# A spectral filter and a gated feed-forward block on one core: written order with a framework scheduler, against an order planned at build time

## The chip, the cores and the metric

One of the eight cores of one Trainium2 chip. The metric is the device time of one execution in microseconds (us); medians are over the executions of a run. "Span" is the time from the first to the last instruction of the profiled execution; in every execution on record it is 1.7 to 1.9 us shorter than the time of that execution. Engine names are those of the profile: PE is TensorE's matmul, PEld its weight load, DVE is VectorE, ACT is ScalarE, POOL is GpSimd, SP is SyncE, which here only issues DMA (SPq is its queue).

## The reference

Inputs are drawn in bfloat16. What matters:

```python
x  = A_x                                     # 1 x 2048 x 640
xn = layernorm(x)                            # over the 640
X  = rfft2(xn) * (w_r + 1j * w_i)            # over both axes
s  = irfft2(X)                               # back to 2048 x 640
g  = silu((gelu(xn @ w_gate) * (xn @ w_up)) @ w_down)   # 640 -> 1536 -> 640
return x + s * g
```

## The kernel before

The 2048 rows are treated as 16 slabs of 128. Each slab is normalised (`stats`, `apply`), turned so that the 640 columns lie on partitions (`turn`), and folded (sums and differences with the mirrored half), which halves the work of the Fourier transform. The transforms are matmuls with small tables. The folded slabs are stored in DRAM and read back regrouped. Then come eight "spectral" steps, a second trip through DRAM (`reload`), and sixteen inverse steps. All this is interleaved with the feed-forward block, which runs in four groups of four slabs: 12 gate/up tiles, then 4 down projections.

The parts that the change touches:

```python
# one slab at a time
def turn(n1, eng=nc.scalar):
    pt = psum.tile([P, 5, P], BF16, tag="sp", name="pt")
    for c in range(5):
        nc.tensor.transpose(out=pt[:, c, :], in_=xn[:, c * P:c * P + P], identity=ident)   # five PE matmuls
    ...                                                       # one evacuation to xnT, ACT or DVE

def fold(n1):
    ...
    nc.vector.tensor_tensor(out=eo[:, 0, :], in0=xn[:, 0:320], in1=xn[:, 639:319:-1], op=ALU.add)
    nc.vector.tensor_tensor(out=eo[:, 1, :], in0=xn[:, 0:320], in1=xn[:, 639:319:-1], op=ALU.subtract)
    ...                                                       # two more of the same size: xf
    nc.tensor.matmul(pa[:, 0, :], lhsT=F1T, rhs=xf[:, :, 0:128], ...)
    nc.tensor.matmul(pa[:, 1, 0:128], lhsT=F1T, rhs=xf[:, :, 128:160], ...)
    nc.scalar.copy(out=A, in_=flat(pa)[:, 0:D])
    nc.sync.dma_start(out=D2[:, n1, :], in_=A)                # store for the regroup

def inverse(n1):                                              # rows of 644 columns
    ...                                                       # 4 matmuls of 128 columns, then
    nc.tensor.matmul(pvf[0:64, 512:640], lhsT=U[:, 256:320], rhs=I1T, ...)
    nc.tensor.matmul(pvf[64:128, 512:640], lhsT=U[:, LP + 257:LP + 321], rhs=I1T, ...)

def down(n1):
    ph = sp_tile("ph")                                        # both halves in one "sp" PSUM tile
    ...                                                       # 24 matmuls of 320 columns, tanh, multiply
# the order is written by hand: what goes with feed-forward step i
for i in range(12):
    after[i].append((norm, 4 + i))                            # stats, apply, turn
    while nf * 12 < (i + 1) * 16:
        after[i].append((fold, nf)); nf += 1
after[11] += [(gather, 0), (gather, 1), (regroup,)]
for G in range(8):
    after[14 + 2 * G].append((spectral_a, G)); after[17 + 2 * G].append((spectral_b, G))
after[31].append((reload,))
...
```

SP and POOL run what they are given in the written order; PE, DVE and ACT get their order from the framework's scheduler, working from this written sequence. PSUM (the matmul outputs) has two slots each of the tags `sp`, `pg` and `pu`.

## Time and profile before

| | before |
|---|---|
| time, median of 3 runs | 235.64 us (235.01 to 235.66) |
| span of the profiled run | 233.3 us |
| granted TensorE clock, mean | 1.000 |
| PE / DVE / ACT busy | 210.0 / 148.6 / 115.9 us |
| first / last matmul starts | 7.9 / 228.4 us |
| matmuls (columns/2.4 + 2.5 ns each), summed | 200.8 us |

The last line needs a word. PE's busy time overstates the array's work, because matmuls overlap in the records. Back to back, a 512-column matmul starts 0.216 us after the one before and a 320-column one 0.136 us, that is columns/2.4 + 2.5 ns. The Trainium skill, "TensorE: Matmul & The Clock Gate", section "Wait — 56ns, not 53.3ns?", gives the same rule, and the trace agrees. I call the sum of it over all matmuls the **stream**: 1428 matmuls, 200.8 us. (The trace holds 1406 of them; the count is the program's.) Then the time can be taken apart: 7.9 us before the first matmul, 200.8 us of stream, some 20 us of **holes** in which nothing streams, 4.7 us after the last matmul.

From the page of the kernel before, the busy table's line and PE's row of 40 slices (busy tenths):

```profile
PE 210.0 (90%) x1406; PEld 122.1 (52%) x1428; DVE 148.6 (64%) x357; ACT 115.9 (50%) x183; POOL 58.9 (25%) x98
...
PE   0588799899999999999999998999999999999972
```

The same by stage, from the windows view of the kernel before (busy us and instructions of each engine in each stretch, then the granted clock, the DMA engines' mean busy share and GB/s):

```profile
core 0: us, PE busy (x) PEld busy (x) DVE busy (x) ACT busy (x) POOL busy (x), PEclk, DMA share, GB/s
0.00:20.00 20.00, 9.99 (x79) 7.21 (x81) 10.60 (x35) 10.18 (x21) 6.63 (x19) 1.00 0.87 282
20.00:60.00 40.00, 36.38 (x224) 17.71 (x225) 30.21 (x97) 26.41 (x46) 16.69 (x32) 1.00 0.67 223
60.00:100.00 40.00, 39.21 (x279) 23.74 (x283) 29.21 (x55) 24.16 (x32) 22.45 (x27) 1.00 0.41 127
100.00:140.00 40.00, 38.95 (x261) 23.91 (x264) 26.50 (x46) 16.94 (x24) 6.17 (x8) 1.00 0.24 69
140.00:180.00 40.00, 38.46 (x268) 22.53 (x272) 24.05 (x61) 18.89 (x30) 4.29 (x8) 1.00 0.37 128
```

The waits view of the kernel before names what PE stood waiting for (total us, times, longest):

```profile
PE pt L270 <- DVE xn L263: 10.6, 7, 7.9
...
PE pa L289 <- DVE xf L287: 1.6, 4, 0.6
...
PE ph L469 <- DVE G_2846 L458: 1.5, 1, 1.5
...
PE pv L404 <- DMA BU<-D_93: 1.1, 1, 1.1
```

The first line holds the start (7.9 us before the first turn) and six further waits of turns for normalised slabs. `pa <- xf` are folds that came late. The 1.5 us is the last down projection, which waits for an `sp` slot; the 1.1 us is the first inverse step waiting for the reload. Without the start, all PE waits that the view lists add up to 9.9 us. The rest of the 20 us it doesn't name.

### The profile page before, as it was taken

To read this page: it belongs to the slowest core of one execution; us is meant where nothing else is said; L and a number is where in the kernel's file an instruction comes from. 1 tells how busy PE (TensorE), PEld (TensorE's weight loads), DVE (VectorE), ACT (ScalarE), POOL (GpSimd) and SP (SyncE) were. 2 spreads that over 40 slices of the span, in tenths; PEclk is the share of its full clock that TensorE was granted. 3 is DMA by queue.
4 is the path that set the end of the run, shared out by engine and by line. 5 is a ranking of instruction groups with operands and counts; after the bars stand their busy time and mean duration, and the time that the engine had idled before them with its cause. 6 is when DMAs were issued, how large, how long until landed. Compare 5 with 4: busy or idle time off the path is not lost. (4 is left out here: it accounts for less than half of the span.)

```text
span 233.3 us, 3865 instructions
## 1 busy us (share of the span) xinstructions
PE 210.0 (90%) x1406; PEld 122.1 (52%) x1428; DVE 148.6 (64%) x357; ACT 115.9 (50%) x183; POOL 58.9 (25%) x98
## 2 busy tenths in 40 slices
PE   0588799899999999999999998999999999999972
PEld 0363344346755556555666643544666654545751
DVE  2659798872239998688957242976654586544372
ACT  4279877474174655865352424745243464443210
POOL 1531413437733486646000000110100010000000
PEclk9999999999999999999999999999999999999999
DMA  6995994824960332326201039251211123000011
GB/s 190 385 340 134 357 377 149 300 88 95 342 212 16 100 101 64 106 88 159 83 3 45 11 91 408 86 154 59 84 46 41 56 70 101 0 0 0 32 61 52
DMA packets 21091, 29.67 MB, mean 127 GB/s; under 512 B 2368, under 2 KB 18640, under 8 KB 20944
## 3 DMA queue, kind: packets, MB, share of 16 engines
q1 hardware_dynamic: 18592, 23.83, 29.9%
q0 software_dynamic: 2336, 5.26, 8.5%
q10 hardware_dynamic: 144, 0.33, 0.4%
q8 instruction: 11, 0.18, 0.3%
q14 instruction: 8, 0.07, 0.1%
HBM read 21.53 MB, written 7.88 MB: 126 GB/s over the span
## 5 line engine op out<-in xcount | busy, mean ns | idle before, releaser
L440 PE MATMUL pg<-xnT,Wg 128*128 128x512 bf16 (+1 forms) x241 | 63.4, 373 | 1.6 <-DVE xnT L272 1.3
L440 PE MATMUL pu<-xnT,Wu 128*128 128x512 bf16 (+1 forms) x237 | 61.0, 372 | 0.7 <-issue 0.2
L469 PE MATMUL ph<-Wd,u 128*128 128x320 bf16 x384 | 53.8, 299 | 2.5 <-DVE G_2846 L458 1.5
L469 PEld LDWEIGHTS <-u 128*128 128x128 bf16 x384 | 37.4, 98 | 18.0 <-issue 3.3
L448 DVE TENSOR_TENSOR u<-pu,ge 128x512 bf16<-128x512 f32 x48 | 32.9, 685 | 9.4 <-PE pu L440 9.1
L446 ACT ACTIVATE ge<-pg 128x512 bf16<-128x512 f32 x48 | 28.9, 602 | 17.9 <-PE pg L440 17.7
L440 PEld LDWEIGHTS <-Wu 128*128 128x128 bf16 x250 | 24.0, 99 | 22.5
L479 POOL DMA_DIRECT2D xr<-in_A_x_dram x16 | 8.7, 548 | 104.9 <-DVE res L485 104.9
L457 ACT ACTIVATE th<-ph 128x640 f32<-128x640 f32 (+1 forms) x17 | 11.4, 673 | 47.3 <-PE ph L469 47.3
L440 PEld LDWEIGHTS <-Wg 128*128 128x128 bf16 x250 | 22.9, 98 | 20.8 <-issue 0.9
L311 POOL DMA_INDIRECT W<-in_A_w_r_dram,LANE x16 | 16.8, 1047 | 6.0 <-POOL W L308 3.5
L311 POOL DMA_INDIRECT W<-in_A_w_i_dram,LANE x16 | 16.0, 1000 | 4.9 <-issue 4.9
L270 PE MATMUL pt<-ident,xn 128*128 128x128 bf16 x80 | 7.4, 231 | 10.6 <-DVE xn L263 10.6
L411 ACT CAST Vt<-pv 128x640 bf16<-128x640 f32 x16 | 11.1, 692 | 9.0 <-PE pv L408 9.0
L272 ACT COPY xnT<-pt 128x640 bf16<-128x640 bf16 x14 | 9.7, 693 | 10.9 <-PE pt L270 10.9
L353 ACT CAST E<-pe 128x644 bf16<-128x644 f32 x16 | 13.1, 890 | 3.4 <-PE pe L351 3.4
L270 PEld LDWEIGHTS <-xn 128*128 128x128 bf16 x80 | 5.2, 103 | 14.6 <-DVE xn L263 14.2
L242 DVE BATCH_NORM_STATS2 st<-X 128x6 f32<-128x320 bf16 x22 | 10.1, 480 | 3.5 <-DMA X<-in_A_x_dram 3.5
L292 ACT CAST A<-pa 128x640 bf16<-128x640 f32 x16 | 11.1, 693 | 2.5 <-PE pa L290 1.1
L255 POOL TENSOR_SCALAR rstd<-mva 128x1 f32<-128x1 f32 x11 | 3.0, 275 | 31.4 <-DVE mva L243 31.3
L356 DVE TENSOR_TENSOR V<-E 128x644 bf16<-128x644 bf16 x8 | 4.0, 495 | 11.0 <-ACT E L353 11.0
L385 PE MATMUL pi<-R,BD 128*128 128x322 bf16 x64 | 10.5, 300 | 0.4 <-DVE R L377 0.4
(177 smaller groups left out, 269.3 us busy)
## 6 DMA issues: line engine op xcount, KB each, us to landing
D_93<-IU SPq DMA_DIRECT2D x8, 322.0 KB, 2.9
BU<-D_93 SPq DMA_DIRECT2D x4, 644.0 KB, 6.2
D_92<-A SPq DMA_DIRECT2D x16, 160.0 KB, 2.2
BU<-D_92 SPq DMA_DIRECT2D x4, 640.0 KB, 6.9
xr<-in_A_x_dram POOLq DMA_DIRECT2D x16, 160.0 KB, 2.5
out_dram<-res SPq DMA_DIRECT2D x15, 160.0 KB, 1.8
Wg<-in_B_w_gate_dram SPq DMA_DIRECT2D x4, 480.0 KB, 7.6
Wu<-in_B_w_up_dram SPq DMA_DIRECT2D x4, 480.0 KB, 7.7
```

The costliest lines, as they stand in the source:

```text
L242: nc.vector.bn_stats(out=st[:, g, :], in_=x[:, 320 * g:320 * g + 320])
L270: nc.tensor.transpose(out=pt[:, c, :], in_=xn[:, c * P:c * P + P], identity=ident)
L292: nc.scalar.copy(out=A, in_=flat(pa)[:, 0:D])
L311: nc.gpsimd.indirect_dma_start(out=W[:, pm, ri, 0:L], out_offset=None, in_=wsrc, in_offset=bass.IndirectOffsetOnAxis(ap=LANE[:, 2 * G + pm ...
L353: nc.scalar.copy(out=E[:, ri].rearrange("p r (i q) -> p r q i", q=2), in_=pe[:, :, 0:LP].rearrange("p r (q i) -> p r q i", q=2))
L385: nc.tensor.matmul(pi[:, pq, 0:LP], lhsT=BD[:, G, ro, ri, :], rhs=R[:, ri, pq, :], start=(ri == 0), stop=(ri == 1))
L411: nc.scalar.copy(out=flat(Vt), in_=pvf[:, 0:D])
L440: nc.tensor.matmul(ps[:, lo:hi], lhsT=w[:, c, t * P:(t + 1) * P], rhs=xnT[:, c, grp * 512 + lo:grp * 512 + hi], start=(c == 0), stop=(c == ...
L446: nc.scalar.activation(out=ge, in_=pg, func=ACT.Gelu_apprx_tanh)
L448: nc.vector.tensor_tensor(out=u, in0=pu, in1=ge, op=ALU.mult)
L457: nc.scalar.activation(out=th[:, a:b], in_=ph[:, a:b, 0:320], func=ACT.Tanh, scale=0.5)
L469: nc.tensor.matmul(ph[:, a, 0:320], lhsT=uT[grp, t][:, j * P:(j + 1) * P], rhs=Wd[:, t, 320 * a:320 * a + 320], start=(t == 0), stop=(t == ...
```

## The change

Its intent: PE's order should never put a matmul in front of data that isn't there yet. All tasks are entered in a list with their costs in ns, their dependencies and their buffers ("slots"); a scheduler in the build runs through simulated time, gives each free engine the ready task of best rank, and the instructions are then emitted in that order, on every engine, with the framework's scheduling off. With it come smaller changes of the operations:

- slabs 4 to 15 are turned by the DMA crossbar (`dma_start_transpose`) in place of five PE matmuls and an evacuation;
- folds and unfolds work on pairs of slabs, half as many DVE instructions of twice the size;
- the inverse rows have 640 columns, so the tail needs one matmul in place of two;
- a down projection is two halves that use `pg` and `pu` slots, not `sp`; an evacuation goes to ACT or DVE, whichever the plan finds free;
- a few more go along: two more slabs' statistics go to ACT, the first two gate/up tiles are done in four parts, and a pair of folds is stored at once.

The core of the diff, cut:

```diff
+class Plan:
+    MARGIN = dict(PE=250, DVE=60, ACT=60, POOL=60, SP=60)
+    ...
+    def run(self):
+        left, now, order = list(self.tasks), 0.0, []
+        while left:
+            ...                                   # ready task of best rank on a free engine, else step time on
+            occ, lat = t.engs[e]
+            self.free[e] = now + occ
+            t.done = now + lat
+            if t.size:                            # a transfer: one shared wire, 340 bytes per ns
+                self.wire = max(self.wire, now + occ + 900) + t.size * t.slow / 340.0
+                t.done = self.wire + 1000
+            ...
+def c_pe(*ns):
+    occ = sum(n / 2.4 + 2.5 for n in ns)
+    return occ, occ + 240
+...
+    BUFS = dict(sp=2, pg=2, pu=2, s1=4, ma=2, mb=2, mc=2, Y=1, ...)
+...
+    def turn_dma(n1, ap):
+        turned[n1] = add(lambda e: nc.sync.dma_start_transpose(out=xnT[:, :, n1 * P:(n1 + 1) * P],
+                                                               in_=sxn.tile[:, n1 % 2, :]),
+                         "SP", (600, 600), (0, -1, n1), after=[ap], use=[sxn], size=163840, slow=1.6)
+    def fold(j, aps):                             # a pair of slabs; outputs mc, one store per pair
+        nc.vector.tensor_tensor(out=eo.tile[:, :, 0, :], in0=sxn.tile[:, :, 0:320], in1=sxn.tile[:, :, 639:319:-1], op=ALU.add)
+        ...
+        stored[j] = dma(lambda: D2[:, 2 * j:2 * j + 2, :], lambda: A.tile, (0, -1, j), 327680, after=outs, use=[A], slow=1.1)
+...
+        (turn_pe if n1 < 4 else turn_dma)(n1, aps[n1])
-    after[31].append((reload,))
-    ...                                           # the written order
+    with tc.manual_schedule():
+        for t in plan.run():
+            t.emit(t.on)
```

## The prediction

It was written before the changed kernel ran.

> **What bounds the kernel now.** TensorE. The page's busy table gives PE 210.0 of 233.3 us (DVE 148.6, ACT 115.9). Busy overstates the array's work: in the chain that ended last, five 512-column matmuls take 1.08 us and 24 of 320 columns 3.26 us, that is columns/2.4 + 2.5 ns each, which agrees with the Trainium skill, "TensorE: Matmul & The Clock Gate", section "Wait — 56ns, not 53.3ns?". Summed over the program this gives an estimated 201 us of stream. The other 32 us: some 11.5 us of delay by 17 us (7.9 before the first PE instruction in the timeline, then slabs' turns); an estimated 8 us between 17 and 60 us, where the windows by stage show PE at 84 to 96%, DVE at 85 to 94%, DMA at 60 to 90%, and PE waits for xn (turns) and xf (folds); 1.1 us at the reload (140 us); small bubbles; 1.5 us in the last down projection, waiting for a PSUM slot; 4.6 us after the last matmul.
>
> **What the change removes.** 60 of 80 PE turn matmuls (60 x 56 ns = 3.3 us of stream), 12 evacuations of 0.69 us, one 128-column matmul per inverse slab (0.9 us). Stream falls to about 196.6 us. Folds on pairs: 64 DVE operations of 0.32 us become 32 of 0.49 us, about -5 us of DVE. Statistics: 2 slabs (about 2 us each) move from DVE to ACT. Down halves use the pg/pu slots, not sp, so the 1.5 us wait goes.
>
> **What it adds.** 12 crossbar turns of 160 KB. The skill, "DMA: Bandwidth & Descriptors", "Latency and other measured facts", gives 261 GB/s: 0.6 us each plus some 2 us to landing; no run here shows it yet. They queue behind all loads (10.8 MB, at the windows' 290 GB/s done near 37 us). Slabs 4-7 are needed only when group 0 is finished, near 57 us, so I expect no wait. The stores for the regroup stand behind the last turns; the regroup is needed near 72 us. Splitting down adds 16 small tanh and multiply operations, off the path.
>
> **The plan's costs** match the trace: successive 644-element DVE operations start 0.41 us apart, 1288-element ones 0.74, u products 0.60. So DVE should keep up with the static order.
>
> **Sum.** PE reaches its first full-width tile at about 17 us as before, with 6.7 us of stream done; 190 remain; stalls and bubbles after that I put at 6 us (the 16 of before less most of the early 8 and the last 1.5); last matmul near 213; tail 4.3; span 217 to 218, plus the 2.3 us between span and time. Predicted **220 us, 213 to 229**; faster by over 2%: 0.90, within 2%: 0.07, slower: 0.03.
>
> **What would show it right.** 20 turn matmuls, 80 inverse first-stage matmuls; PE busy near 201 us or below; PE at 95% or more in every window from 20 to 60 us; no wait of gate/up for xnT by DMA; no PE gap at the regroup; the last down without a gap.
>
> **What would make it wrong.** Crossbar turns far slower than 160 KB per 1 us, or holding the queue, so that group 1 waits for xnT or the first spectral matmul for the regroup (a 5 to 15 us PE gap near 57 or 72 us); PE waiting in order for R or evacuations in the spectral and inverse stages, if the greedy plan packs them too closely (3 to 5 us); a later start.

## The result, and the profile after

| | before | after |
|---|---|---|
| time, median of 4 runs each, same chip | 235.39 us | 217.77 us (217.3 to 219.55) |
| ratio | | 0.9269 (95%: 0.9229 to 0.9308) |
| span | 233.3 us | 216.1 us |
| first / last matmul starts | 7.9 / 228.4 us | 8.3 / 210.9 us |
| stream | 200.8 us | 196.6 us |
| holes between first and last matmul | 19.8 us | 6.2 us |
| after the last matmul | 4.7 us | 5.0 us |

A ratio is the mean time of one kernel's fast runs over that of the other's of the same rounds, so it is not quite the ratio of the medians quoted. Executions over 1.5% slower than the fastest of the same kernel are left out of the means. The span's gain of 17.2 us is 4.2 us of stream and 13.6 us of holes (2.6 of them the inverse tail's, see e1r_pe_turns), less 0.3 us of later start and 0.3 us of longer tail.

From the page of the changed kernel:

```profile
PE 200.2 (93%) x1392; PEld 123.2 (57%) x1392; DVE 146.3 (68%) x304; ACT 113.0 (52%) x192; POOL 59.0 (27%) x95
...
PE   0499999996999999999999999999999999999991
```

Its windows view, in the same stretches:

```profile
0.00:20.00 20.00, 11.22 (x116) 9.30 (x117) 14.06 (x39) 12.41 (x26) 10.52 (x33) 1.00 0.95 302
20.00:60.00 40.00, 37.77 (x220) 20.80 (x218) 30.70 (x68) 18.39 (x37) 18.14 (x27) 1.00 1.03 259
60.00:100.00 40.00, 40.00 (x282) 23.79 (x280) 25.41 (x46) 21.10 (x30) 8.22 (x7) 1.00 0.29 93
100.00:140.00 40.00, 40.00 (x265) 24.21 (x264) 29.39 (x56) 25.29 (x39) 15.13 (x16) 1.00 0.38 109
140.00:180.00 40.00, 40.00 (x337) 27.68 (x336) 32.29 (x72) 27.01 (x46) 6.43 (x12) 1.00 0.47 157
```

From 60 us to 180 us the view shows no gap of PE. DVE has 146.3 us of work where it had 148.6, and ACT 113.0 where it had 115.9, so the other engines do hardly less; whether the gain is the order's, the experiments must tell. What remains is the digit 6 in PE's row, a hole at 51 us, with a small one at 56 us. The PE timeline of the changed kernel around it (start, duration, then in brackets the idle time and its releaser):

```profile
50.24 0.98 PE L793 MATMUL pu<-Wd,uT 128*128 128x320 bf16 x6
53.12 0.38 PE L470 MATMUL sp<-mb,F1T 128*128 128x512 bf16 x1 [1.90 <-ACT mc L301]
...
56.60 0.38 PE L470 MATMUL sp<-mb,F1T 128*128 128x512 bf16 x1 [0.34 <-ACT mc L301]
```

A fold matmul waits for ACT to free a PSUM slot by evacuating into `mc`. Its waits view says what ACT waited for, and shows one wait near the end:

```profile
ACT mc L301 <- DMA D<-mc: 7.3, 3, 3.7
...
PE sp L470 <- ACT mc L301: 2.2, 2, 1.9
...
DVE ge L817 <- ACT th L802: 1.1, 1, 1.1
```

`mc` has two buffers, and ACT waits until an earlier one has been stored. The timeline of SP's queue in the changed kernel shows where these stores were:

```profile
35.16 8.89 SPq L434 DMA_TRANSPOSE xnT<-s  x6
44.15 0.53 SPq L308 DMA_DIRECT2D D<-mc  x1
44.77 2.58 SPq L434 DMA_TRANSPOSE xnT<-s  x2
47.44 0.53 SPq L308 DMA_DIRECT2D D<-mc  x1
48.06 3.00 SPq L434 DMA_TRANSPOSE xnT<-s  x2
51.16 8.20 SPq L308 DMA_DIRECT2D D<-mc  x4
```

They stood behind crossbar turns. The 16 DMA engines were full at that time, too: in the windows view their busy share between 40 and 50 us is 1.10, and 0.23 in e1r_pe_turns, which has no crossbar turns. So a turn costs its queue and the DMA engines, and the runs below don't separate the two. The changed kernel's view of the turn's line gives its price: duration on the queue as min/median/max, and the time from issue to landing.

```profile
L434 SPq DMA_TRANSPOSE xnT<-s x12: 1227/1250/2228, 31.0 to 49.5; - x12
...
DMA to landing us min/median/max: 3.6/5.2/6.1
```

The plan had reckoned with 600 ns of the queue and 0.77 us of the wire (163,840 bytes times 1.6 over 340).

### The profile page after: what moved, and what is told of

The parts are those of the page before. It is cut to its first block, busy times and chain, and to the rows that moved or that the text cites. A ratio compares the mean times of both kernels' runs of the same rounds, so it can differ in the third digit from the quotient of the medians.

```text
span 216.1 us, 3756 instructions
## 1 busy us (share of the span) xinstructions
PE 200.2 (93%) x1392; PEld 123.2 (57%) x1392; DVE 146.3 (68%) x304; ACT 113.0 (52%) x192; POOL 59.0 (27%) x95
## 4 chain that ended last, share of the span: by engine, by line
PE 89%; DMA 4%; DVE 3%; ACT 2%; issue 1%; SPq 0%; ACTq 0%
PE pg L750 24%; PE pu L750 24%; PE pg L793 11%; PE pu L793 10%; PE sp L650 4%; DMA D<-mc 2%; PE sp L587 2%; PE sp L683 2%; PE sp L696 2%; PE sp L583 2%; PE sp L693 2%; DMA X<-in_A_x_dram 2%; PE sp L566 2%; PE sp L470 1%; DVE STAT L382 1%; PE sp L416 1%
## 5 line engine op out<-in xcount | busy, mean ns | idle before, releaser
L766 DVE TENSOR_TENSOR uT<-pu,ge 128x512 bf16<-128x512 f32 x48 | 32.9, 688 | 40.5 <-PE pu L750 34.9
L793 PEld LDWEIGHTS <-uT 128*128 128x128 bf16 x384 | 36.3, 98 | 13.3
L793 PE MATMUL pg<-Wd,uT 128*128 128x320 bf16 (+1 forms) x192 | 31.6, 301 | 0.0
L793 PE MATMUL pu<-Wd,uT 128*128 128x320 bf16 (+1 forms) x192 | 31.0, 297 | 0.0
L526 POOL DMA_INDIRECT WF<-in_A_w_r_dram,LANE x16 | 17.3, 1083 | 41.7 <-DVE mc L622 37.2
L301 ACT CAST ma<-sp 128x644 bf16<-128x644 f32 (+1 forms) x32 | 24.1, 794 | 4.8 <-PE sp L696 2.6
L526 POOL DMA_INDIRECT WF<-in_A_w_i_dram,LANE x16 | 16.0, 999 | 4.9 <-issue 4.6
L301 ACT CAST IU<-sp 128x640 bf16<-128x640 f32 x16 | 10.9, 693 | 3.3 <-PE sp L650 2.2
L301 ACT CAST Vt<-sp 128x640 bf16<-128x640 f32 x15 | 10.4, 692 | 4.1 <-PE sp L683 4.1
L650 PE MATMUL sp<-R,BD 128*128 128x320 bf16 x64 | 11.1, 300 | 0.0
```

The costliest lines, as they stand in the source:

```text
L301: return nc.scalar.copy(out=out, in_=in_) if e == "ACT" else nc.vector.tensor_copy(out=out, in_=in_)
L526: nc.gpsimd.indirect_dma_start(out=sw.tile[:, pm, ri, 0:L], out_offset=None, in_=wsrc, in_offset=bass.IndirectOffsetOnAxis(ap=LANE[:, 2 * ...
L650: nc.tensor.matmul(pt[:, pq, 0:320], lhsT=BD[:, G, ro, ri, :], rhs=sR.tile[:, ri, pq, pq:pq + 320], start=(ri == 0), stop=(ri == 1))
L766: nc.vector.tensor_tensor(out=u.tile, in0=pu.tile, in1=ge.tile, op=ALU.mult)
L793: nc.tensor.matmul(ps.tile[:, 0:hi - lo], lhsT=uT[grp, t].tile[:, j * P:(j + 1) * P], rhs=Wd[:, t, lo:hi], start=(t == 0), stop=(t == 11))
```

## The experiments

Theory 1: the gain is the planned order with realistic durations; the new operations matter less, and the crossbar turns hardly at all, because the hole at 51 us gives back what they save. Rival 2: the cheaper operations make the gain, and the old order with them would do nearly as well. Rival 3: any static order with enough buffers does it; the timing is beside the point.

The trials used several chips. On chip 14 the kernel before takes what it took at first (235.3 and 235.9 us; one of its executions took 564.91 us and is left out of the ratios). On chips 7 and 8 it takes 242.4 and 244.5 us, and every kernel traced there has stretches in which PE is slow; those runs are told too, but carry little.

### On chip 7: four kernels, three rounds each

**e1_pe_turns** turns all slabs on PE again:

```diff
-        (turn_pe if n1 < 4 else turn_dma)(n1, aps[n1])
+        turn_pe(n1, aps[n1])
```

> The changed kernel with all 16 slabs turned on the TensorE again (evacuated by ACT or DVE as the plan likes), the plan made anew. Theory O (the timed order closes the holes; the crossbar only takes 60 matmuls off the TensorE and costs the 2.5 us hole near 51 us, where stores stand behind turns in the SP queue): 217.8 + 3.3 - 2.5 = about 218.6 us, range 217.5 to 220, with under 1 us of TensorE holes after 20 us. Theory L (the lighter work closes the holes: without PE turns ACT, DVE, PSUM slots and TensorE are free in the first 60 us): 222 us or more, with several us of holes again between 20 and 60 us.

Measured: 235.93 us, ratio to before 0.9750 (0.9708 to 0.9792).

**e2_plan_old_ops** keeps the plan, turns all slabs on PE and also takes back the pairs and the single tail matmul: each pair operation becomes two per slab, with costs to match, and the tail is two matmuls again:

```diff
-            nc.vector.tensor_tensor(out=eo.tile[:, :, 0, :], in0=sxn.tile[:, :, 0:320], in1=sxn.tile[:, :, 639:319:-1], op=ALU.add)
+            for q in range(2):
+                nc.vector.tensor_tensor(out=eo.tile[:, q, 0, :], in0=sxn.tile[:, q, 0:320], in1=sxn.tile[:, q, 639:319:-1], op=ALU.add)
 # ... and so for all eight fold and unfold operations
-                for c in range(5):
+                for c in range(4):
 # ...
+                for q in range(2):
+                    nc.tensor.matmul(pt[64 * q:64 * q + 64, 512:640], lhsT=U[:, 256 + 64 * q:320 + 64 * q], rhs=I1T, ...)
```

> The plan with the old operations: all turns on the TensorE, every fold and unfold operation of a pair split into two of one slab (64 + 64 operations of 320 elements as before), six matmuls in the inverse's first stage. Only the order, the buffers and the split down projection are then new. Theory O: 217.8 + 3.3 + 0.9 - 2.5 = 219.5 to 221 us. Theory L: 226 us or more, most of the way back to 235.

Measured: 243.99 us, ratio 1.0052 (0.9993 to 1.0111).

**e3_before_new_ops** is the kernel before, in its written order, with the new operations: crossbar turns, pairs, 640-column rows, down halves in `pg`/`pu`:

```diff
     def turn(n1, eng=nc.scalar):
         xn = xn_of[n1]
+        if n1 >= 4:
+            return nc.sync.dma_start_transpose(out=xnT[:, :, n1 * P:(n1 + 1) * P], in_=xn)
 # ... fold and unfold on pairs, five inverse matmuls:
-        ph = sp_tile("ph")
+        for a, tag in ((0, "pg"), (1, "pu")):
+            ph = psum.tile([P, 512], FP32, tag=tag, name=tag)
```

> The kernel before, in its own written order, with the new operations: crossbar turns from slab 4, folds and unfolds on pairs, 640-column rows with five matmuls, the down projection in two halves on the gate/up PSUM slots. Theory O: the stream falls by the same 4.1 us, the 1.5 us wait of the last down projection goes, the other holes mostly stay: 226 to 231 us. Theory L: 220 us or less.

Measured: 234.86 us, ratio 0.9699 (0.9666 to 0.9732).

**e4_mc4** is the changed kernel with four `mc` buffers (`mc=2` to `mc=4`), against the hole.

> The changed kernel with four instead of two buffers for the folds' results (the tiles that the stores to DRAM read, which stand behind crossbar turns in the SP queue), the plan made anew. Theory O: the TensorE hole of 2.1 + 0.5 us at 51 to 57 us closes, 215.3 us, range 214.8 to 216.2. Rival: the stores' lateness itself sets the time, the hole only moves to the regroup: 217.8 us as now.

Measured: 231.13 us, ratio 0.9520 (0.9469 to 0.9571); one of its four executions (235.31 us) was slow.

All four came out slower than the same or the nearest kernel did elsewhere, and so did the kernel before, by 7 us. Their traces have stretches (about 45 to 68 us and, in three of the four, 100 to 136 us) where PE's matmuls and weight loads come some 0.7 us or more apart, with nothing to wait for; the timeline of e4_mc4 shows it:

```profile
48.57 0.30 PE L793 MATMUL pu<-Wd,uT 128*128 128x320 bf16 x1 [1.68 <-issue]
48.59 0.10 PEld L793 LDWEIGHTS <-uT 128*128 128x128 bf16 x1 [1.32 <-issue]
...
49.28 0.30 PE L793 MATMUL pu<-Wd,uT 128*128 128x320 bf16 x1 [0.41 <-issue]
```

"issue" means that the profile shows no wait. It is not every engine: in this stretch ACT and DVE do nothing until it is over, but POOL's gathers of the filter weights keep their pace of one in 1.25 us. The granted clock also fell to half in or after such stretches (from 50.7 to 57.6 us in e4_mc4). In all these traces, and in e8_turn_cost_only, each stretch begins during a run of twelve or more such gathers and ends at most 5 us after it (e4_mc4: gathers from 36.2 to 51.3 us, stretch from 47 to 55 us). On chip 14 the same runs of gathers pass without one, so this is a lead and no cause: what causes the stretches stays open. Since they hit the kernels in different places, I don't compare these four.

### On chip 14: the same question again

**c1_after** is the changed kernel unaltered, as a control.

> Control: the changed kernel unaltered, because the last four runs were on a chip on which the kernel before took 242.4 us instead of 235.4[...]. If this chip is like the first: 217.8 us and a ratio to before of 0.927. If it is like the second: ratio near 0.95 and the same stretches.

Measured: 217.74 us, ratio 0.9206 (0.9116 to 0.9295; the interval is wide because it rests on three fast executions of 215.31, 217.61 and 217.87 us; the fourth, 219.09, counts as slow). The hole is there: 1.9 us at 48.1 us and 1.1 us at 52.2 us.

**e2r_plan_old_ops**, the plan with the old operations.

> The plan with the old operations once more, beside the control. Theory O (order closes the holes): 2 to 3 us over the control, 219.5 to 221 us on a chip like the first. Theory L (lighter work closes them): 9 us or more over the control.

Measured: 222.24 us, ratio 0.9452 (0.9410 to 0.9494). That is 4.5 us over the control: more than theory O gave (2 to 3), and half of what theory L asked for (9 or more). Where the extra comes from is told at e1r_pe_turns. From its page, PE's row:

```profile
PE   0589999999999999999999999999999999999990
```

DVE and ACT have more work here than in the kernel before (152.7 and 116.8 us against 148.6 and 115.9), and yet PE has no single hole above 0.4 us after 20 us. So it isn't lighter work that closes the holes.

**e3r_before_new_ops**, the old order with the new operations.

> The old order with the new operations once more, beside the control. Theory O: 226 to 231 us on a chip like the first, 8 to 13 us over the control. Theory L: at most 3 us over it. (On the second chip it was 0.970 of before.)

Measured: 230.54 us, ratio 0.9799 (0.9755 to 0.9843), as theory O had it; whether it is a full 2% faster than before stays unclear. From its page PE's row, and from its waits view:

```profile
PE   0488878888979899999999998999999999999992
```

```profile
PE pa L301 <- DVE xf L296: 6.7, 8, 1.1
...
PE pzt L334 <- DMA BU<-D: 1.3, 1, 1.3
```

All eight pairs of folds now hold PE for about a microsecond each, where before four of the single folds held it for 1.6 us in all. The pair operations are cheaper for DVE, but a pair is ready later, and the order had not been adapted. The two runs and the two kernels themselves make a table of two by two (us):

| | old operations | new operations |
|---|---|---|
| old order | 235.3 | 230.5 |
| planned order | 222.2 | 217.7 |

The order is worth 12.8 to 13.0 us, the operations 4.5 to 4.7 us, and the two add. Rival 2 is refuted. (The columns aren't perfectly clean: the down halves in `pg`/`pu` stayed in the upper right and the lower left kernel, so the removal of the last down's 1.5 us gap counts with whichever came first. And "planned order" stands for all that the plan decides: the order on every engine, the buffers, and which engine takes an evacuation or a slab's statistics. How much each of these is worth isn't separated.)

**e6_all_four** tries four repairs on the changed kernel at once: `mc=4`; the plan's first load landing later (`self.wire` 2200 to 4400 ns); fifteen matmuls on a zero tile before the data arrive, and statistics of slabs 3 to 5 held back so that the first turns come first; the last down's twelve matmuls in one piece per half.

```diff
-        self.wire = 2200.0
+        self.wire = 4400.0
-    BUFS = dict(..., mc=2, ...)
+    BUFS = dict(..., mc=4, ...)
+        pw = psum.tile([P, 512], FP32, tag="pg", name="pg")
+        for _ in range(15):
+            nc.tensor.matmul(pw, lhsT=WARM[:, 0:P], rhs=WARM, start=True, stop=True, ...)
-            for k in range(0, 12, 6):
+            for k in range(0, 12, step_k):            # 12 for the last down
```

> The changed kernel with four edits at four places, to be read one by one in the trace: (1) four buffers for the folds' results: the hole of 2.1 + 0.5 us at 51 to 57 us goes; (2) 15 matmuls on a tile of zeros before the first slab, so that the TensorE is at full clock when the first turns come: the 3.4 us at half speed after 10 us go, 1.0 to 1.8 us; (3) the first slab normalised before the fourth slab's statistics, and the plan told the measured time of the first loads: first turn 0.5 to 0.8 us earlier; (4) the last down projection one column half after the other: tail 0.5 to 0.9 us shorter. Sum: 4 to 6 us under the control, about 213 us on a chip like the first. If starting earlier is worth nothing because DVE sets the pace until 18 us, (2) and (3) together give under 0.5 us.

Measured: 213.86 us, ratio 0.9088 (0.9051 to 0.9126), so 3.9 us below the control. In its trace the hole at 51 us is gone, but a new one of the same size came at 62 us; the PE timeline of e6_all_four:

```profile
61.56 1.24 PE L752 MATMUL pg<-xnT,Wg 128*128 128x512 bf16 x5
64.50 1.07 PE L568 MATMUL sp<-T,BU 128*128 128x128 bf16 x16 [1.70 <-DMA BU<-D]
```

With more `mc` buffers the plan believed that the stores, and so the regroup, would be done much earlier, and put the first spectral matmuls 8.6 us of stream earlier than in the changed kernel (5.4 us if the fifteen matmuls on the zero tile, 3.2 us, are counted in). But the stores still stood behind turns that take longer than the plan thought. The wait had moved to the next step that depended on the same wrong number. (The profiled execution was the slowest of six, 215.52 us; four took 213.5 to 213.9 us, and whether they had this hole isn't known.) The start did improve: five 128-column matmuls start 0.28 us after one another from the first, where the changed kernel needs 0.53 us until 13.4 us, and the first full-width gate tile comes at 16.0 us in place of 18.3.

### On chip 14: the turns, the timing, the turn's cost (five rounds each)

**e1r_pe_turns**, all turns on PE, planned.

> The changed kernel with all turns on the TensorE, once more, hopefully on a chip like the first. Crossbar alone: it takes 3.3 us of matmuls away and brings the hole of 2.0 to 2.6 us near 50 us, so undoing it costs 0.7 to 1.3 us: 218.5 to 219 us, ratio to before about 0.930, with no hole over 0.5 us after 20 us. If the crossbar also frees what keeps the TensorE fed: 221 us or more.

Measured: 217.84 us, ratio 0.9244 (0.9216 to 0.9272): the same as the changed kernel, and a little under the 218.5 to 219 expected. With 3.3 us more of matmuls it has no hole above 0.25 us after 20 us. The crossbar turns are worth nothing here: what they save on PE comes back as a hole of 2.5 to 3 us.

This run also tells what the other operations are worth. It differs from e2r_plan_old_ops only in the pairs and in the tail of the inverse step, and is 4.4 us faster. The PE timelines of e2r_plan_old_ops and then of e1r_pe_turns, one inverse step each:

```profile
150.39 0.39 PE L685 MATMUL sp<-I1T,BU 128*128 128x128 bf16 x4
150.71 0.25 PE L688 MATMUL sp<-I1T,BU 128*64 128x128 bf16 x2
150.88 0.99 PE L804 MATMUL pu<-Wd,uT 128*128 128x320 bf16 x6
...
149.91 0.44 PE L683 MATMUL sp<-I1T,BU 128*128 128x128 bf16 x5
150.19 0.98 PE L793 MATMUL pu<-Wd,uT 128*128 128x320 bf16 x6
```

Four full matmuls and two with 64 columns of weights (`128*64`) hold PE for 0.50 us, five full ones for 0.28 us. The two half ones start 4 ns after one another, but 0.15 us pass before the pair and 0.18 us after it. The kernel before shows the same 0.50 us in its inverse steps. So one matmul in place of two is worth 0.217 us a slab and 3.5 us in all: 0.9 us of stream, as predicted, and 2.6 us of what the sum of the stream leaves in the holes. This is read from the trace; a run with the tail alone changed was not made. It is most of the 4.5 us that the operations are worth under the planned order.

**e5_untimed** keeps the plan's mechanism, ranks and buffers, but lies to it about the durations: every task of an engine costs the same, and transfers take 2 us whatever they move and whatever else is under way.

```diff
-            occ, lat = t.engs[e]
+            occ, lat = {"PE": (900, 1140), "DVE": (500, 620), "ACT": (800, 940), "POOL": (1000, 1150), "SP": (430, 430)}[e]
-                self.wire = max(self.wire, now + occ + 900) + t.size * t.slow / 340.0
-                t.done = self.wire + 1000
+                t.done = now + occ + 2000
```

> The changed kernel planned by the same scheduler with the same priorities, dependences and buffers, but without the timing: every task of an engine counts as equally long (TensorE 0.9, DVE 0.5, ACT 0.8, POOL 1.0 us), every transfer lands 2 us after its issue, however large. If the durations matter to the plan: TensorE holes of several us come back, 224 to 232 us. If any greedy order over this graph does as well: within 2 us of 217.7.

Measured: 265.34 us, ratio 1.1261 (1.1222 to 1.1300), slower than the kernel before. I had expected a loss and not one of this size. From its page PE's row and the granted clock (tenths), and from its waits view the worst chain:

```profile
PE   0145106596887888788999999999999999999992
...
PEclk9999757779999999999999999999999999999998
```

```profile
ACT mc L300 <- DMA D<-mc: 19.0, 3, 13.0
PE sp L469 <- ACT mc L300: 18.2, 4, 12.9
```

The plan, which thought that every transfer landed in 2 us, put the early folds' matmuls in PE's order as if their stores would pass at once. In the trace the first store of a folded pair is issued at 35.7 us, behind all loads and three turns. PE stood for 13 us behind one evacuation, and the array's clock fell to half in and after the idle spells (the 5 and 7 of the clock row). The Trainium skill, "TensorE: Matmul & The Clock Gate", section "Part 1: The HAM clock gate (the "warmup" mystery)", says that the array is throttled to half rate by default and that sustained activity releases it; this trace agrees, with a mean granted clock of 0.957. Rival 3 is refuted as far as it says "any": this order has the same ranks and buffers and is slower than the hand-written one. This one kernel changes all durations at once, those of the transfers too; how much each lie costs isn't separated, though the largest hole is the transfers'.

**e7_turn_cost** is e6_all_four with the measured cost of a turn in the plan:

```diff
-                         "SP", (600, 600), (0, -1, n1), after=[ap], use=[sxn], size=163840, slow=1.6)
+                         "SP", (1300, 1300), (0, -1, n1), after=[ap], use=[sxn], size=163840, slow=2.7)
```

> The kernel with four edits (213.9 us) with the plan told what a crossbar turn costs in the trace: 1.3 us of the SP queue and 1.3 us of transfer, not 0.6 and 0.8. In that run a new hole of 1.87 us stood at 62.4 us, ahead of the first spectral matmul, which the plan had put 5 us too early because it believed the turns and the stores behind them to be done sooner. Told the cost it puts that matmul 3.3 us of TensorE work later; the hole goes, 212.0 us, range 211.3 to 212.8. If the hole is not the plan's belief but the transfers themselves, it moves and the time stays at 213.9.

Measured: 213.69 us, ratio 0.9065 (0.9039 to 0.9090). In its trace the hole at 62 us is gone, as expected: after 20 us PE has no hole above 0.25 us, and the first spectral matmuls now stand 3.2 us of stream later than in e6_all_four. But the time missed the 211.3 to 212.8 us expected: the median fell by only 0.2 us, which can't be told from nothing. One reason is in the trace, since the plan's first 15 us came out otherwise as well. Another may be that the faster executions of e6_all_four did not have the hole. What this repair is worth in time isn't shown. From its waits view:

```profile
PE pg L752 <- ACT ge L764: 1.8, 1, 1.8
```

The first full-width gate tile stands at 15.4 us behind a Gelu on ACT, and ACT's timeline shows why: between 13.5 and 16.8 us it works through statistics passes (0.72 and 0.83 us each) that the plan placed ahead of that Gelu. A change of one cost can reshuffle the whole order. With e6_all_four this is the fastest version measured.

### On chip 8: the last one

**e8_turn_cost_only** is the changed kernel with `mc=4` and the turn's cost of e7_turn_cost, and nothing of the other start, to see whether the hole at 51 us goes without replacement.

> The changed kernel with two edits alone: four buffers mc in place of two for the folded matmul outputs that wait to be stored, and a crossbar turn costed in the plan at 1.3 us of the SP queue (0.6 before) and 1.3 us of the wire (0.77). No warm-up matmuls, no other start, no other last down. Theory A (the 2.5 to 3 us of PE gaps near 51 and 56 us in the changed kernel came only from the plan's too cheap turn, with stores standing behind turns, and the gap at 15 us in the last run belongs to the changed start there): no PE gap above 0.5 us after 20 us, last matmul start near 208.3, 215.0 to 215.8 us, ratio 0.912 to 0.916 to before. Rival B (removing that hole moves the wait elsewhere again, as it did twice): a new gap of 1.5 us or more somewhere after 20 us, and 216.8 to 218 us, ratio 0.920 or more.

Measured: 233.83 us (228.4 to 235.09) where the kernel before took 244.45; five of its six runs, the profiled one among them, were slow (span 232.2 us, clock 0.962), and no ratio of use came out. The trace has the same stretches as on chip 7, at 47 to 55 and 103 to 113 us, with 15.2 and 13.1 us of PE busy in the 20 us around them. Outside them PE has no hole above 0.25 us after 20 us, and no PE wait for `mc` or for the regroup is listed. That fits the first expectation. But one stretch lies just where the hole had been and gave the stores more time, so it isn't shown: the question stays open, and so does how much of e6's gain comes from each of its four repairs.

## Why the prediction was right

220 us was predicted and 217.8 measured, inside the range. Term by term, as the sum in the prediction had them:

- **Stream 196.6 us.** Measured 196.6: the changed trace records all 1392 matmuls. But one of its parts was undersized: the single matmul in the inverse tail, put at 0.9 us, is worth 3.5 (e1r_pe_turns).
- **First full-width tile near 17 us with 6.7 us of stream done**, a delay of 10.3 us. Measured: that tile came at 18.3 us, and at 20 us the delay was 11.7 us (8.3 to the first matmul, 3.4 of holes). The term was 1.4 us too small. The half-speed array of the first 13.4 us is part of it. (The spacing of the matmuls shows it, 0.53 us for five of 128 columns; the clock column reads 1.00 there, but the trace's first clock record comes only at 13.7 us.) How long it lasts varies: in c1_after, the same kernel, the first record comes at 11.8 us and that tile at 17.7. And e6_all_four, which warms it, is 2.3 us earlier, but that kernel changes the start in another way too.
- **Stalls of 6 us after that.** This term failed most. Measured 2.8 us, nearly all at 51 and 56 us. I had trusted that the plan's costs match the trace and yet left 6 us for imperfection. From 60 us on PE had no gap at all, 40.00 of 40.00 in three windows.
- **Last matmul near 213 us.** Measured 210.9 (196.6 + 11.7 + 2.8 = 211.1 for its end).
- **Tail 4.3 us.** Measured 5.0. DVE stood 1.1 us before its multiply by y, with ACT's tanh on the same PSUM tile as releaser; for the first 0.6 us of it that tile's matmuls were still running, so the tanh cost at most 0.6 us. I had put the tail a little below the 4.7 us of before.
- **2.3 us between span and time.** Measured 1.8, and 1.7 to 1.9 in every execution. The 2.3 set the median of three runs of the kernel before against the span of the profiled one, which by that must have taken some 235.1 us.

The mechanism was right: the waits for turns and folds between 20 and 60 us, for the reload and for the last down's slot went away, and the experiments put about three quarters of the gain (12.8 to 13.0 of 17.6 us) on the order. It was also right that the DVE would keep up.

Of the signs that were to show it right one failed: PE was to be at 95% or more in every window from 20 to 60 us, and it had 7.77 us of the ten from 50 to 60 us. It is the hole at 51 us, and behind it one statement was wrong: "so I expect no wait" from the crossbar turns, and with it "no PE gap at the regroup" as far as the stores before it go. I had asked whether gate/up would wait for turned slabs, and they did not. But I took an estimate of 0.6 us each from the Trainium skill, "DMA: Bandwidth & Descriptors", section "Latency and other measured facts" (261 GB/s), and the turns held the queue for 1.25 us each and landed after 5.2 us; stores behind them came late, which held ACT, which held a PSUM slot, which held PE. The risk stood in the list ("holding the queue"), but with the wrong victim and 5 to 15 us; it cost some 2.5 us. For this reason the crossbar turns, which I counted as 3.3 us of saving, brought nothing net (e1r_pe_turns).

## What to carry to other kernels

When PE is the bound and its gaps are small and many, look for the gain in the order, and work it out with durations measured in the trace; a static order built on wrong ones was slower here than the loose hand-written order (265 against 236 us). A wrong cost shows as a wait at the next step that depends on it: repair the number in the plan, not only the buffer where the wait shows, or it moves on (so it was in the traces of e6_all_four and e7_turn_cost; what the last repair is worth in time isn't shown). And an operation moved to a DMA queue must be costed for what stands behind it in that queue, not only for its own result. Last, a rule that adds up matmuls can hide a cost: two half-width matmuls were 0.217 us dearer here than one full one, and no view listed that as a wait.

## What the Trainium skill lacked or had wrong

- "DMA: Bandwidth & Descriptors", "Latency and other measured facts": 261 GB/s for a DMA transpose (an estimate of 0.6 us for 160 KB) wasn't seen. Successive turns from SBUF to SBUF, with other transfers under way, took 1.25 us of the queue each (131 GB/s, with the DMA engines' busy share at 1.10 from 40 to 50 us) and 5.2 us from issue to landing. For a turn of this shape the page has no figure of how long it holds its issuing queue (its table in the section on trn3 B0 has cycles of the sequencer for earlier chips, of another size).
- "TensorE: Matmul & The Clock Gate", "Wait — 56ns, not 53.3ns?": agreed for full matmuls. From 58.8 us to the last matmul of the changed kernel, where PE has no gap, 1063 of them should take 151.9 us by the rule, and took 152.2.
- The same page, "Part 1: The HAM clock gate (the "warmup" mystery)": the half rate at the start agreed (0.53 us for five 128-column matmuls, then 0.28). That matmuls on an all-zero tile release it isn't said there; fifteen of them from 1.2 to 6.3 us did in e6_all_four, whose first record of the full clock comes at 4.6 us.
- I found on no page the stretches of chips 7 and 8, in which PE's instructions come some 0.7 us apart with nothing to wait for. On chip 7 they went with 7 us more for the kernel before, 4 us for it with the new operations, and 18 and 22 us for two planned kernels (235.93 and 243.99 us against 217.84 and 222.24 on chip 14).
- On no page did I find what a change from full weights to 64 columns of weights and back costs in time (it would belong to "TensorEngine Tiling (Array Packing)"). Here 0.15 us passed before a pair of such matmuls and 0.18 us after it, where full ones follow after 0.056 us.
